# Windowed attention into a dropless MoE: one product a head for the values, and a different order of the copies and the routing around them

## The chip, the cores and the metric

One core of a Trainium2 chip runs the whole program. The metric is device time in microseconds of one execution; lower is better. Times come from separate runs, and one further execution was taken with the hardware profiler. Everything is float32.

## The reference, cut to what matters

```python
# attention: B, H, S, D = 4, 8, 768, 64; 8 memory keys a head; chunks of 32 queries
for c in range(S // 32):                 # each chunk sees its own 32 keys,
    l, r = max(0, 32*c - 16), min(S, 32*c + 32 + 8)   # 16 before, 8 behind
    k_full = concat(mem_k, k[:, :, l:r]); v_full = concat(mem_v, v[:, :, l:r])
    a = softmax(q_c @ k_full.T / sqrt(D))
    out[:, :, c] = a @ v_full
x = out.transpose(0, 2, 1, 3).reshape(B * S, H * D)    # 3072 tokens of 512
# mixture of experts: 8 experts, 512 -> 1024 -> 512
logits = x @ w_gate
e = argmax(logits); gate = softmax(logits)[e]
y[token] = gate * (relu(x[token] @ w1[e]) @ w2[e])
```

## The kernel before

**Stages.** Attention runs over 32 blocks `i` of 96 queries (8 blocks a batch entry). Behind it the last tokens are routed, while TensorE works on the first 256 tokens of expert 0 (`ph`, `py`), and then the eight experts follow, one after another, to the end. The change lies in the attention stage, in the first 140 us or so of the program.

**A block.** The 96 queries of a block see a window of 128 columns of `kT` (keys and the memory keys, which are copied in between). TensorE makes, in this order and written out by hand (`tc.manual_schedule`, one loop over `i` from line 1172):

1. `turn_q(i + 2)`: four transposes of q into a bank of PSUM (`tqk<-cst,qn`, line 544), then two copies by ScalarE into `qT` (line 661). Two blocks share one load of q: an even call turns the even heads of the pair of blocks, an odd call the odd heads. So what block `i` turns at an odd `i` is needed by the scores of block `i + 1`.
2. `scores(i)`: 16 products of 64 by 64 weights (`sc`, line 539), with keys on the partitions and queries along the row, then three exponentials by ScalarE, one for each chunk of 32 queries, into `ex` (line 713). `sc` has one buffer, so the next scores wait for these exponentials.
3. `values(i - 1, 0)` and `values(i - 1, 1)`: four heads each. The weights are the columns of `ex` (one per query), `v` with a column of ones is streamed (65 columns), and `o` gets the sums and the divisor. A head's 96 queries are taken as two products of 64 columns each (c = 0, 1), to partitions 0 to 63 and 64 to 127 of the bank. The second reaches 32 columns past the head, so `ex` is one tile with 32 zeroed columns at its end, in two fixed buffers, and the last 32 partitions of the bank aren't used. VectorE takes the reciprocal (line 730) and multiplies (line 732) into `xr`, the block's rows of x.
4. `turn_xb(i - 2)`: four transposes of x (`tx`) and a copy by ScalarE into a slice of a weight buffer (`w<-tx`, line 739), for the logits.
5. `turn_k(i + 4)`: four transposes of k (`tqk<-cst,kn`) and two copies by VectorE into `kT` (line 679; line 683 for the memory keys of a new batch entry).

Every four or five blocks (`GROUPS`) the logits of a finished group are made in the midst of the values (`o<-w,wg`), and its routing is put on a list `work` of small steps for VectorE (`top` to `where`), one product pair for TensorE (`rank`), the multiplication of x by the gate (GpSimd, line 843, for the first 22 blocks) and the scatters. `routing(n)` takes up to `n` VectorE steps from that list at its place in the block: 3 between the two halves of the values and 5 at the end of the block while i is below 24. A scatter (line 875, GpSimd, one per block of tokens) writes the rows of x to their experts' places in `x_dram`. Each is issued behind the TensorE instruction that stood last when it was written. `xr` has `NXR` = 12 buffers, and a block writes the one that the scatter of 12 blocks before has read.

**Queues.** SyncE issues all loads of q, k and v, in an order written out by hand three to six blocks ahead. Its waits are for buffers. A float32 product is two loads of weights and two matmuls in the trace; a transpose is one of each.

Of the kernel before, what the change touches and what calls it, by code (L numbers as in the profile page):

```python
# [10 lines left out]
F32 = mybir.dt.float32  # L11
# [8 lines left out]
B, H, S, D = 4, 8, 768, 64  # L20
NMEM = 8
CHUNK, LEFT, RIGHT = 32, 16, 8
QB = 96
NQB = S // QB
NB = B * NQB
# [43 lines left out]
PAIRS = QB  # L69
# [23 lines left out]
SIDE = max(t1 - t0 for t0, t1 in GROUPS)  # L93
EARLY = 22
BY_POOL = 22
NXR = 12


def can_be_plain(e):
# [433 lines left out]
def ordinary(ctx, tc, q, k, v, mem_k, mem_v, moe_w_gate, moe_w1, moe_w2, out, good):  # L533

    nc = tc.nc
    cur = {}

    def mm(*args, **more):
        i = nc.tensor.matmul(*args, **more)  # L539
        cur["pe"] = i.ins.name  # L540
        return i
# [18 lines left out]
    kpool = actx.enter_context(tc.tile_pool(name="kpool", bufs=1))  # L560
# [31 lines left out]

    qTs = [kpool.tile([128, H // 2, 2 * QB], F32, name=f"qT{i}") for i in range(NQ)]

    exs = [kpool.tile([128, H * QB + CHUNK], F32, name=f"ex{i}") for i in range(2)]
    for t in exs:
        nc.vector.memset(t[:, H * QB :], 0.0)
    vs = [kpool.tile([128, H, DV], F32, name=f"v{i}") for i in range(NV)]
    for t in vs:
        nc.gpsimd.memset(t[:, :, D], 1.0)  # L600
# [24 lines left out]
    sbs = [dict() for _ in range(NSB)]  # L625
# [21 lines left out]
    def turned_heads(t, n, x, bank=None):  # L647
        if bank is None:
            tt = ps_t.tile([128, H // 2, n], F32, tag="t", name="tqk")
        else:  # L650
            tt = bank[:, 0 : H // 2 * n].rearrange("p (a n) -> p a n", a=H // 2)
        for a in range(H // 2):
            turn(tt[:, a], t[0:n, 2 * a + x], ident[0:n, 0:n])
        return tt

    def turn_q(m, copy=nc.scalar.copy, bank=None):
        j, x = divmod(m, 2)
        tq = turned_heads(sbs[j]["qn"], PAIRS, x, bank)
        to = sbs[j]["qT"][D * x : D * x + D].rearrange("d a (p t) -> d a p t", t=2)
        for t in range(2):  # L660
            copy(to[:, :, :, t], tq[D * t : D * t + D])  # L661

    def turn_k(m, copy=nc.vector.tensor_copy, bank=None):
        j, x = divmod(m, 2)
        b, s = divmod(j, NSB // B)
        if s == 0 and x == 0:
            turned[b] = apool.tile([128, H // 2, KW], F32, name="kT")
        n = PAIRS + NMEM // 2 if s == 0 else PAIRS
        tk = turned_heads(sbs[j]["kn"], n, x, bank)
        half = turned[b][D * x : D * x + D]  # L670
        for t in range(2):
            of = tk[D * t : D * t + D]
            to = half[:, :, 2 * PER * s + t : 2 * PER * s + 2 * PER]
            to = bass.AP(
                tensor=to.tensor,
                offset=to.offset,
                ap=[list(to.ap[0]), [KW, H // 2], [PER, 2], [QB // 2 + NMEM, 2], [2, QB // 4]],
            )
            i = copy(to, of[:, :, 0:PAIRS].rearrange("d a (y z p) -> d a y z p", y=2, z=2))  # L679
            keyed.setdefault((b, s), []).append(i.ins.name)  # L680
            if s == 0:
                to = half.rearrange("d a (y c) -> d a y c", y=NQB)[:, :, :, QB // 2 : QB // 2 + NMEM]
                copy(
                    to.rearrange("d a y (p t) -> d a y p t", t=2)[:, :, :, :, t], bc(of[:, :, PAIRS:], 2, NQB)
                )

    def scores(i):
        s, (b, qb) = st[i], divmod(i, NQB)
        w0 = window(qb)
        sc = ps_s.tile([128, 2, 512], F32, tag="s", name="sc")  # L690
        for a in range(H // 2):
            for c in range(0, WIN, 64):
                for x in range(2):
                    rows = slice(D * x, D * x + D)
                    ins = mm(
                        sc[c : c + 64, x, QB * a : QB * a + QB],
                        lhsT=turned[b][rows, a, w0 + c : w0 + c + 64],
                        rhs=sbs[i // 2]["qT"][rows, a, QB * (i % 2) : QB * (i % 2) + QB],
                        start=True,
                        stop=True,  # L700
                    )
                    for z in range(NQB // 2):
                        if not w0 // (2 * PER) <= z <= (w0 + WIN - 1) // (2 * PER):
                            for j in keyed.get((b, z), []):
                                tc.declare_no_dep(ins.ins, j, reason="other keys")
        s["ex"] = exs[i % 2]
        ex = s["ex"][:, 0 : H * QB].rearrange("p (h t) -> p h t", h=H)
        x = 0 if qb == 0 else 2 if qb == NQB - 1 else 1
        sc4 = sc[:, :, 0 : 4 * QB].rearrange("p g (h t) -> p g h t", h=4)
        ex4 = ex.rearrange("p (h g) t -> p g h t", g=2)  # L710
        for g in range(3):
            sl = slice(CHUNK * g, CHUNK * g + CHUNK)
            nc.scalar.activation(  # L713
                ex4[:, :, :, sl], sc4[:, :, :, sl], AF.Exp, bias=mask[:, 3 * x + g : 3 * x + g + 1], scale=D**-0.5
            )

    def values(i, g, bank):
        s = st[i]
        if g == 0:
            s["x"] = xr[:, i % NXR, LB:DX]  # L720
        full = bank[:, 0 : 4 * (D + 1)].rearrange("p (h d) -> p h d", h=4)
        o = full[0:QB]
        for j in range(4):
            h = 4 * g + j
            for c in range(2):
                of = s["ex"][:, QB * h + 64 * c : QB * h + 64 * c + 64]
                mm(full[64 * c : 64 * c + 64, j], lhsT=of, rhs=s["v"][:, h, 0 : D + 1], start=True, stop=True)

        inv = inv_all[:, i, 4 * g : 4 * g + 4]
        nc.vector.reciprocal(inv, o[:, :, D])  # L730
        x = s["x"].rearrange("p (h d) -> p h d", h=H)
        nc.vector.tensor_tensor(x[:, 4 * g : 4 * g + 4], o[:, :, 0:D], bc(inv, 2, D), op=OP.mult)
# [170 lines left out]
    def routing(n, kinds="v"):  # L903
        while work and (n and work[0][0] in kinds or work[0][0] == "b"):
            kind, f = work.pop(0)
            f()
            n -= kind not in "sb"
# [6 lines left out]
    def scatter_some(n):  # L914
        while spread and n:
            spread.pop(0)()
            n -= 1

    def need(i, f, *lists):
        if 0 <= i < NB:  # L920
            f(i)
# [231 lines left out]
    with tc.manual_schedule():  # L1153
# [18 lines left out]
        for i in range(NB):  # L1172
            if i // 2 + 3 < NSB:
                (load_k, load_q)[i % 2](i // 2 + 3)
            need(i + 3, load_v)
            if i > 0:
                need(i + 2, turn_q)
            scores(i)
            if i == 0:
                need(i + 2, turn_q)  # L1180
            scatter_some(1)
            banks = [ps_o.tile([128, 512], F32, tag="o", name="o") for _ in range(2)]
            cur["bank"] = banks[0]
            if i <= 23:
                routing(1, "p")
            early_cnt = None
            if len(scatters) >= EARLY and "early" not in cur:
                cur["early"] = i
                early_cnt = early_counted(banks[0])
            if i >= 1:  # L1190
                values(i - 1, 0, banks[0])
            if early_cnt is not None:
                early_count(early_cnt)
            routing(5 if i > 23 else 3)
            done = [g for g in range(len(GROUPS)) if i - 3 == GROUPS[g][1] - 1]
            late = logits(done[0], banks[1]) if done else None
            if i >= 1:
                values(i - 1, 1, banks[1])
            need(i - 2, turn_xb)
            if late:  # L1200
                place_logits(*late)
            if i > 23:
                routing(1, "p")
            scatter_some(1)
            if i >= 24:
                routing(6)
            for m in {0: (), 1: (4, 5)}.get(i, (i + 4,)):
                need(m, turn_k)
            if i < 24:
                routing(5)  # L1210
            hold_back()
            for g in done:
                work.extend(routed(g))
            if i == 24:
                fetch_w(0, 4)
            if i >= 24:
                fetch_piece(1)
                fetch_piece(1)
            if i == 5:
                behind(  # L1220
                    nc.gpsimd.dma_start(
                        x_dram[0:TAIL].rearrange("(x p) c -> p x c", x=2), bc(zeros.bitcast(I32), 1, 2)
                    )
                )
                behind(nc.gpsimd.dma_start(x_dram[TAIL:NER], zeros[0 : NER - TAIL].bitcast(I32)))
            if i == 29:
                early_load()
                early_gather()
# [801 lines left out]
```

## Time and profile before

| | |
|---|---|
| timed runs | 470.24, 470.84, 476.84 us; median 470.84 |
| profiled execution | 474.63 us, of which the span is 472.5 |
| mean granted TensorE clock | 0.98 |
| TensorE busy | 439.4 us (93% of the span) |
| VectorE, ScalarE, GpSimd busy | 297.5, 195.3, 175.8 us |
| 60 to 120 us, per 20 us: TensorE | 17.66, 17.89, 19.05 us busy |
| the same: ScalarE | 13.30, 13.62, 14.23 us busy |
| the same: VectorE | 15.04, 15.15, 15.57 us busy |

A row of a profile that is in order of time has the start, the length, the engine, the line, the operation, out<-in, the shape (rows by columns of the weights, then partitions by streamed columns) and how many records were merged; in brackets stands an idle time of the engine before it and what ended it. PE is the matmul, PEld the load of weights that lies over it. "issue" is idle time in which the engine waited for nothing that the profile shows. The length of a matmul holds its way through the array, so the step between two rows is read from their starts.

### The profile page before, as it was taken

How to read it: one execution, taken by the hardware profiler on the slowest of the kernel's cores; microseconds unless marked ns; L12 is line 12 of the kernel's file. 1: busy time of each engine (PE TensorE's matmuls, PEld its weight loads, DVE VectorE, ACT ScalarE, POOL GpSimd, SP SyncE). 2: the span in 40 equal slices, each digit the busy share in tenths (PEclk: the TensorE clock that was granted, in tenths of full speed). 3: DMA queues.
4: the chain of work that ended last, by engine and by line, in shares of the span. 5: the costliest groups of instructions: out<-in, count | busy, mean ns of one | idle time of the engine just before them, and what ended most of it. 6: DMA issues, size and time to landing. Idle time of an engine off the chain costs nothing. (4 is left out here: it accounts for less than half of the span.)

```text
span 472.5 us, 11804 instructions
## 1 busy us (share of the span) xinstructions
PE 439.4 (93%) x4412; PEld 393.8 (83%) x4412; DVE 297.5 (63%) x572; ACT 195.3 (41%) x369; POOL 175.8 (37%) x211
## 2 busy tenths in 40 slices
PE   4799997999999899999999999999999999899992
PEld 4687786887778769999899999977888998879991
DVE  3476686787377586885476777765537977556410
ACT  3587675676532136421352254134213622135211
POOL 1010947877553206721414552232122333240124
PEclk9899999999799999999999999999999999999997
DMA  9999999999975686768895896594614979824002
GB/s 197 184 202 231 215 263 232 244 280 273 289 196 184 237 243 178 226 136 256 236 273 134 250 290 163 179 281 122 192 44 121 244 209 259 249 78 103 15 24 92
DMA packets 142239, 92.42 MB, mean 196 GB/s; under 512 B 79621, under 2 KB 125134, under 8 KB 142160
## 3 DMA queue, kind: packets, MB, share of 16 engines
q1 hardware_dynamic: 127504, 64.55, 57.5%
q10 hardware_dynamic: 7744, 13.24, 9.0%
q0 software_dynamic: 6912, 13.54, 8.2%
q8 instruction: 54, 0.88, 0.8%
q14 instruction: 25, 0.20, 0.2%
HBM read 65.68 MB, written 21.28 MB: 184 GB/s over the span
## 5 line engine op out<-in xcount | busy, mean ns | idle before, releaser
L1521 POOL DMA_INDIRECT out_dram<-y,lab x41 | 44.6, 1087 | 112.9 <-PE sum_q L539 43.6
L966 POOL DMA_INDIRECT lab<-x_dram,rows x42 | 52.0, 1239 | 65.0 <-PE sum_q L539 27.6
L539 PE MATMUL sum_p<-xsT,w 128*128 128x320 f32 (+8 forms) x256 | 53.7, 354 | 3.0 <-issue 1.9
L539 PEld LDWEIGHTS sum_p<-xsT,w 128*128 128x128 f32 x256 | 42.8, 190 | 9.8 <-issue 4.6
L539 PE MATMUL o<-v,ex 128*64 128x65 f32 x1024 | 43.7, 232 | 4.8 <-issue 4.8
L539 PEld LDWEIGHTS o<-v,ex 128*64 128x64 f32 x1024 | 36.4, 143 | 11.6 <-issue 8.5
L713 ACT ACTIVATE ex<-sc,cst 128x256 f32<-128x256 f32 x96 | 38.5, 471 | 12.9 <-PE sc L539 5.3
L1438 ACT COPY sum_r<-sum_p 128x640 f32<-128x640 f32 x36 | 24.4, 677 | 46.0 <-PE sum_p L539 40.1
L875 POOL DMA_INDIRECT x_dram<-xr,dest x32 | 29.9, 933 | 25.0 <-PE o L539 7.6
L539 PE MATMUL sum_q<-t,s 128*128 128x140 f32 (+5 forms) x192 | 36.7, 339 | 1.9 <-ACT sum_r L1438 1.9
L679 DVE COPY kT<-tqk 64x384 f32<-64x384 f32 x60 | 33.2, 554 | 7.9 <-PE tqk L544 6.7
L539 PE MATMUL sum_r<-t,w 128*128 128x140 f32 (+5 forms) x192 | 36.8, 339 | 0.0
L539 PE MATMUL sum_p<-t,s 128*128 128x140 f32 (+5 forms) x192 | 36.6, 339 | 0.0
L539 PEld LDWEIGHTS sum_q<-t,s 128*128 128x128 f32 x192 | 31.8, 193 | 5.5 <-issue 2.8
L539 PE MATMUL sum_p<-h,w 128*128 128x140 f32 (+5 forms) x192 | 35.6, 339 | 0.0
L730 DVE RECIPROCAL inv_all<-o 96x4 f32<-96x4 f32 x64 | 11.7, 183 | 37.4 <-PE o L539 27.6
L843 POOL TENSOR_SCALAR xr<-xr 96x512 f32<-96x512 f32 x22 | 34.1, 1557 | 0.2 <-DVE inv_all L730 0.2
L539 PEld LDWEIGHTS sum_p<-t,s 128*128 128x128 f32 x192 | 31.9, 193 | 2.2
L539 PEld LDWEIGHTS sum_p<-h,w 128*128 128x128 f32 x192 | 31.9, 195 | 2.2 <-issue 0.2
L539 PEld LDWEIGHTS sum_r<-t,w 128*128 128x128 f32 x192 | 31.8, 193 | 2.2
L661 ACT COPY qT<-tqk 64x384 f32<-64x384 f32 x60 | 30.4, 506 | 7.3 <-PE tqk L544 6.5
L1485 DVE STREAM_TRANSPOSE h<-yT 128x640 f32<-128x640 f32 x28 | 23.6, 841 | 14.7 <-DMA y<-h 14.2
(186 smaller groups left out, 800.7 us busy)
## 6 DMA issues: line engine op xcount, KB each, us to landing
w<-in_moe_w_dram SPq DMA_DIRECT2D x128, 128.0 KB
w<-in_moe_w_dram ACTq DMA_DIRECT2D x6, 2048.0 KB
xs<-x_dram SPq DMA_DIRECT2D x56, 160.0 KB
y<-h SPq DMA_DIRECT2D x112, 80.0 KB
kn<-in_k_dram SPq DMA_DIRECT2D x16, 384.0 KB
qn<-in_q_dram SPq DMA_DIRECT2D x16, 384.0 KB
x_dram<-zeros SPq DMA_DIRECT2D x8, 396.0 KB
v<-in_v_dram SPq DMA_DIRECT2D x24, 128.0 KB
```

The source lines that it names most:

```text
L539: i = nc.tensor.matmul(*args, **more)
L661: copy(to[:, :, :, t], tq[D * t : D * t + D])
L679: i = copy(to, of[:, :, 0:PAIRS].rearrange("d a (y z p) -> d a y z p", y=2, z=2))
L713: nc.scalar.activation(ex4[:, :, :, sl], sc4[:, :, :, sl], AF.Exp, bias=mask[:, 3 * x + g : 3 * x + g + 1], scale=D**-0.5)
L730: nc.vector.reciprocal(inv, o[:, :, D])
L843: return lambda: eng.tensor_scalar(x[:, LB:DX], x[:, LB:DX], x[:, 1:2], None, op0=OP.mult)
L875: i = nc.gpsimd.indirect_dma_start(out=x_dram, out_offset=bass.IndirectOffsetOnAxis(ap=dest[:, t : t + 1], axis=0), in_=xr[:, t % NXR].bit ...
L966: return nc.gpsimd.indirect_dma_start(out=to.bitcast(I32), out_offset=None, in_=x_dram.rearrange("r (k c) -> (r k) c", c=LB), in_offset=ba ...
L1438: op("ACT", one_op(lambda: nc.scalar.copy(to, of)), reads, writes)
L1485: op("DVE", one_op(lambda: nc.vector.transpose(to, of)), [("y", m, y)], [("yr", m, y), "y00"], upto=upto)
L1521: return nc.gpsimd.indirect_dma_start(out=out, out_offset=bass.IndirectOffsetOnAxis(ap=which.bitcast(I32), axis=0), in_=y, in_offset=None, ...
```

## The change

- In `values`, a head's 96 queries are one product with 96 columns of weights instead of two with 64. `ex` becomes an ordinary tile of a pool with two buffers, without the zeroed end.
- `turn_q` is split. The transposes stay where they were, before the scores; the two copies (`keep_q`) are written behind the block's exponentials.
- In `turn_k`, of an odd call from the seventh on, the second of the two key copies goes to ScalarE.
- `routing` takes 2 and 3 steps a block instead of 3 and 5 while i is below 24.
- `xr` has 14 buffers.

```diff
-NXR = 12
+NXR = 14
...
-    exs = [kpool.tile([128, H * QB + CHUNK], F32, name=f"ex{i}") for i in range(2)]
-    for t in exs:
-        nc.vector.memset(t[:, H * QB :], 0.0)
...
     def turn_q(m, copy=nc.scalar.copy, bank=None):
+        keep_q(m, turned_heads(sbs[m // 2]["qn"], PAIRS, m % 2, bank), copy)
+
+    def keep_q(m, tq, copy=nc.scalar.copy):
         j, x = divmod(m, 2)
-        tq = turned_heads(sbs[j]["qn"], PAIRS, x, bank)
...
-            i = copy(to, of[:, :, 0:PAIRS].rearrange("d a (y z p) -> d a y z p", y=2, z=2))
+            eng = nc.scalar.copy if t and m % 2 and m > 5 else copy
+            i = eng(to, of[:, :, 0:PAIRS].rearrange("d a (y z p) -> d a y z p", y=2, z=2))
...
-        s["ex"] = exs[i % 2]
-        ex = s["ex"][:, 0 : H * QB].rearrange("p (h t) -> p h t", h=H)
+        ex = s["ex"] = apool.tile([128, H, QB], F32, name="ex")
...
-        full = bank[:, 0 : 4 * (D + 1)].rearrange("p (h d) -> p h d", h=4)
-        o = full[0:QB]
+        o = bank[0:QB, 0 : 4 * (D + 1)].rearrange("p (h d) -> p h d", h=4)
         for j in range(4):
             h = 4 * g + j
-            for c in range(2):
-                of = s["ex"][:, QB * h + 64 * c : QB * h + 64 * c + 64]
-                mm(full[64 * c : 64 * c + 64, j], lhsT=of, rhs=s["v"][:, h, 0 : D + 1], start=True, stop=True)
+            mm(o[:, j], lhsT=s["ex"][:, h], rhs=s["v"][:, h, 0 : D + 1], start=True, stop=True)
...
-            if i > 0:
-                need(i + 2, turn_q)
+            tq = None
+            if 0 < i < NB - 2:
+                tq = turned_heads(sbs[(i + 2) // 2]["qn"], PAIRS, i % 2)
             scores(i)
             if i == 0:
                 need(i + 2, turn_q)
+            if tq is not None:
+                keep_q(i + 2, tq)
...
-            routing(5 if i > 23 else 3)
+            routing(5 if i > 23 else 2)
...
             if i < 24:
-                routing(5)
+                routing(3)
```

On TensorE, from the end of block 7 on, there stands before:

```order
L544 MATMUL tx<-cst,xr 128x96 x4
L544 MATMUL tqk<-cst,kn 128x96 x4
L544 MATMUL tqk<-cst,qn 128x96 x4
L539 MATMUL sc<-qT_102,kT 64x96 x16
L539 MATMUL o<-v_109,ex_105 64x65 x16
L544 MATMUL tx<-cst,xr 128x96 x4
L544 MATMUL tqk<-cst,kn 128x96 x4
L544 MATMUL tqk<-cst,qn 128x96 x4
```

and with the change:

```order
L544 MATMUL tx<-cst,xr 128x96 x4
L544 MATMUL tqk<-cst,kn 128x96 x4
L544 MATMUL tqk<-cst,qn 128x96 x4
L539 MATMUL sc<-qT_102,kT 64x96 x16
L539 MATMUL o<-v_105,ex 96x65 x8
L544 MATMUL tx<-cst,xr 128x96 x4
L544 MATMUL tqk<-cst,kn 128x96 x4
L544 MATMUL tqk<-cst,qn 128x96 x4
```

(64x65 and 96x65 are partitions by columns of the result.) The order of TensorE's steps is the same, the products for logits and ranks included; 16 products of a block's values have become 8.

On ScalarE, blocks 9 to 11, before (`ex` the exponentials, `qT` the copies of q, `w<-tx` the copy of x):

```order
L739 COPY w_131<-tx 128x4x96
L661 COPY qT_103<-tqk 64x384 x2
L713 ACTIVATE ex_105<-sc,cst 128x2x4x32 x3
L739 COPY w_131<-tx 128x4x96
L661 COPY qT_102<-tqk 64x384 x2
L713 ACTIVATE ex_104<-sc,cst 128x2x4x32 x3
L739 COPY w_131<-tx 128x4x96
L661 COPY qT_102<-tqk 64x384 x2
L713 ACTIVATE ex_105<-sc,cst 128x2x4x32 x3
```

and with the change:

```order
L712 ACTIVATE ex<-sc,cst 128x2x4x32 x3
L660 COPY qT_103<-tqk 64x384 x2
L735 COPY w_127<-tx 128x4x96
L679 COPY kT<-tqk 64x4x2x2x24
L712 ACTIVATE ex<-sc,cst 128x2x4x32 x3
L660 COPY qT_102<-tqk 64x384 x2
L735 COPY w_127<-tx 128x4x96
L712 ACTIVATE ex<-sc,cst 128x2x4x32 x3
L660 COPY qT_102<-tqk 64x384 x2
```

In each block the copies of q have moved from in front of the exponentials to behind them, and every second block has a key copy behind the copy of x.

## The prediction

> **What bounds the kernel now.** I read the page first (engine shares), then the attention stage alone, because every edit lies in it: the waits in its window, one undisturbed block of it in order of time, and one disturbed block.
>
> ```profile
> span 472.5 us, 11804 instructions
> PE 439.4 (93%) x4412; PEld 393.8 (83%) x4412; DVE 297.5 (63%) x572; ACT 195.3 (41%) x369; POOL 175.8 (37%) x211
> ```
>
> PE is the bound of the whole. In time order, one block of attention (block 14, from its scores `sc` to the next block's):
>
> ```profile
> 63.75 0.89 PE L539 MATMUL sc<-qT,kT 64*64 64x96 f32 x32
> 64.57 1.15 PE L539 MATMUL o<-v,ex 128*64 128x65 f32 x32
> 65.66 0.55 PE L544 MATMUL tx<-cst,xr 96*128 96x96 f32 x4
> 66.04 0.49 PE L544 MATMUL tqk<-cst,kn 96*128 96x96 f32 x4
> 66.37 0.49 PE L544 MATMUL tqk<-cst,qn 96*128 96x96 f32 x4
> 66.80 0.31 PE L539 MATMUL sc<-qT,kT 64*64 64x96 f32 x4
> ```
>
> First column start, second length. No row has an idle bracket: PE runs 0.82 us of scores, 1.09 of values (`o`), 0.38, 0.33 and 0.43 of transposes, 3.05 us a block, and waits for nobody. So here a longer or shorter PE row moves the block by as much. ScalarE in the same block:
>
> ```profile
> 64.20 1.02 ACT L661 COPY qT<-tqk 64x384 f32<-64x384 f32 x2
> 65.25 1.20 ACT L713 ACTIVATE ex<-sc,cst 128x256 f32<-128x256 f32 x3
> 66.33 0.49 ACT L739 COPY w<-tx 128x384 f32<-128x384 f32 x1
> ```
>
> It has 2.71 us of work in 3.05. The waits of the stage, by the window 10 to 145:
>
> ```profile
> PEld o L539 <- issue: 11.6, 28, 1.6
> PEld tqk L544 <- issue: 4.1, 6, 2.4
> PE tqk L544 <- DMA qn<-in_q_dram: 2.2, 1, 2.2
> PEld tx L544 <- issue: 1.6, 3, 0.7
> PE sc L539 <- ACT ex L713: 0.3, 1, 0.3
> ```
>
> Columns: total us, times, longest. TensorE hardly waits for ScalarE (0.3) and for VectorE not at all; what it loses is "issue", time in which no semaphore holds it. Of 4.1 + 1.6 + 11.6, the one of 2.4 is the load of q shown below it, and the seven logits steps have a regular idle of about 0.25 each (1.7). About **13 us of stalls** are left. What they look like, in block 17:
>
> ```profile
> 75.83 0.49 PE L544 MATMUL tqk<-cst,qn 96*128 96x96 f32 x4
> 75.87 0.99 POOL L875 DMA_INDIRECT x_dram<-xr,dest  x1 [0.17 <-POOL xr L843]
> 76.26 0.89 PE L539 MATMUL sc<-qT,kT 64*64 64x96 f32 x32
> 77.08 0.45 PE L539 MATMUL o<-v,ex 128*64 128x65 f32 x7
> 77.16 0.92 POOL L875 DMA_INDIRECT x_dram<-xr,dest  x1 [0.30 <-issue]
> 77.87 0.38 PE L539 MATMUL o<-v,ex 128*64 128x65 f32 x5 [0.35 <-issue]
> 77.89 0.22 PEld L539 LDWEIGHTS o<-v,ex 128*64 128x64 f32 x4 [0.50 <-issue]
> 78.64 0.82 PE L539 MATMUL o<-v,ex 128*64 128x65 f32 x20 [0.39 <-issue]
> 79.39 0.30 PE L544 MATMUL tx<-cst,xr 96*128 96x96 f32 x1
> ```
>
> In the middle of a group, where nothing is waited for, TensorE gets some 8 instructions (4 loads, 4 products) in 0.76 us and then runs on; `o` takes 2.31 us (77.08 to 79.39) for 1.09. It looks like a shortage of instructions. The stall begins just behind a scatter of GpSimd (77.16) that meets the densest stretch of code; the scatter at 75.87, among transposes, cost nothing.
>
> **The change, part by part.** *Values, one product a head.* Each head had two products with 64 columns of weights, side by side; it gets one with 96 columns. Each product is two records of load and two of matmul, so a block's 32 + 32 records become 16 + 16. The trace shows both widths in one place, at full clock: the small late logits load 96 columns and stream only 8.
>
> ```profile
> 139.92 0.82 PE L539 MATMUL o<-wg,w 128*96 128x8 f32 x8
> 140.66 0.69 PE L539 MATMUL o<-v,ex 128*64 128x65 f32 x16
> 141.28 0.48 PE L539 MATMUL ph<-x0T,w 128*128 128x256 f32 x1
> 139.89 0.76 PEld L539 LDWEIGHTS o<-wg,w 128*96 128x96 f32 x8
> 140.66 0.55 PEld L539 LDWEIGHTS o<-v,ex 128*64 128x64 f32 x16
> L539 PEld LDWEIGHTS o<-wg,w x24: 159/165/165, 139.9 to 148.5; 128*96 128x96 f32 x24
> L539 PEld LDWEIGHTS o<-v,ex x992: 132/138/232, 20.0 to 141.1; 128*64 128x64 f32 x199
> ```
>
> Eight loads of 96 columns fill 0.76 us with the last one's 0.165 in it: a step of (0.76 - 0.165)/7 = **0.085 us**. Sixteen of 64 step (0.55 - 0.138)/15 = 0.0275, so a pair takes 0.055. A group of four heads, entry and exit included, took 0.62 (140.66 to 141.28) with 16 narrow records; eight wide ones took 0.74 (139.92 to 140.66), of which 0.74 - 7 x 0.085 = 0.145 is the way in and out. Sixteen wide records in a row are then 15 x 0.085 + 0.145 = 1.42 us against 1.09: **+0.33 a block**. What has no row is a 96-column load with 65 columns streamed. Its bounds: nothing (the wide step equals the pair's) and 2 x 0.74 - 1.09 = +0.39; I take +0.33, by the nearest row. There are 32 blocks of values; the first lies under the load of q that PE waits 2.2 us for, so 31 x 0.33 = **+10.2 us** (0 to +12.5).
>
> A rule of the skill bears on this price. The Trainium skill, "TensorE: Matmul & The Clock Gate", section "LDWEIGHTS (loading the stationary operand)", has a load last its columns over 1.2 in ns, whatever the rows. By it 96 columns cost an estimated 80 ns against 53 for 64 that run side by side, which speaks against the change, and the sum by it (27 ns a step, 15 steps, 31 blocks) would be 1.4 us below mine; the row above agrees to 5 ns.
>
> *Fewer instructions against the stalls.* The scores ask for 64 instructions in 0.82 us and the values for 64 in 1.09, 59 per us; after the change the values ask for 32 in 1.42, 23 per us. Transposes ask for 8 in 0.33, 24 per us, and it was among transposes that the scatter cost nothing. Values should become as patient as these; the scores stay dense. A block's instructions fall from 152 (64, 64, and 24 for transposes) to 120. Bounds: 0 (a stall is a fixed outage) and -13 (all go). A scatter that falls before or into the scores still finds the queue drained there, so I take seven tenths, **-9.2 us**.
>
> *The clock.* A slow stretch follows the stalls of 122 to 125:
>
> ```profile
> 116.70:125.20 8.50, 7.39 (x171) 5.95 (x170) 4.04 (x11) 4.92 (x11) 6.95 (x6) 1.00 1.02 277
> 125.20:132.00 6.80, 6.79 (x105) 5.89 (x105) 3.44 (x18) 3.27 (x8) 1.87 (x6) 0.50 0.62 205
> 125.87 1.56 PE L539 MATMUL sc<-qT,kT 64*64 64x96 f32 x32
> 127.87 2.00 PE L539 MATMUL o<-v,ex 128*64 128x65 f32 x32
> 129.80 0.90 PE L544 MATMUL tx<-cst,xr 96*128 96x96 f32 x4
> 130.63 1.54 PE L539 MATMUL sc<-qT,kT 64*64 64x96 f32 x32
> ```
>
> In the first two rows the column behind the five engines is the granted clock: 0.50 for 6.8 us, after a stretch in which PE idled 1.1 us. Against the lengths in the undisturbed block the two scores cost 0.67 and 0.65 more, the values 0.85, the transposes 0.35: 2.5 us. If the stalls ahead of it shrink, it need not come. I take two thirds, **-1.7** (0 to -2.5; a new drop elsewhere would cost as much).
>
> *q's copies behind the exponentials; a key copy in four by ScalarE.* Now the exponentials wait for the copies (64.20 to 65.22) though the scores ended at 64.64. Swapped, they can run from about 64.74 to 65.94, and the copies to 66.96. In every odd block those copies are the half of q that the next block's scores need; TensorE, with 1.42 for the values, gets there at 66.80 + 0.33 = 67.13. They stay covered, by 0.17 us; if that cover goes, the next scores wait, some 0.1 us in 15 blocks, 1.5 in all. Queued behind them are `w` (0.49) and, in odd blocks, the key copy (about 0.5); the next exponentials need ScalarE at 67.13 + 0.98 = 68.11, and it is done at about 67.9. I take 0 (0 to +1.5).
>
> *Routing over more blocks, 14 buffers.* VectorE's small steps move back by up to a block, but TensorE's rank products and GpSimd's scatters stay in the same blocks. PE waits for neither engine in the list above, so 0; the early part of the first expert, which follows without a gap, starts as much earlier or later as attention ends.
>
> **Sum**: +10.2 - 9.2 - 1.7 + 0 = -0.7 us. The profiled execution took 474.63 us (472.5 of span, 2.1 around it), so it would take 473.9. It is 3.8 above the median of the three timed runs, 470.84; the difference put on the median gives 470.1, and I say **470**. (The timed runs may hold fewer of the stalls than the profiled one, and so have less to win; that lies inside the range.) Two per cent of 470.84 is 9.4 us, about what a measurement of this kernel can tell from no change.
>
> **The rivals.** *S, slower: the stalls don't care for density.* If each is a fixed outage behind a scatter, the rarer instructions wait just as long, the slow clock comes too, and the wide loads are paid in full: +10.2, so 481.0. For it: stalls also stand in front of transposes (the 4.1 and 1.6 above). Against it: the free scatter at 75.87. It decides as soon as less than a tenth of the 13 us goes. The Trainium skill, "Runtime: NRT & Kernel Launch", section "Instruction fetch mechanics", says that code streams in by blocks and that crossing one is mostly hidden; by that rule thinner code buys nothing, which is this rival's result. The gaps inside a group speak against it.
>
> *F, faster: the wide load is cheaper than the row.* Transposes load 128 columns quicker:
>
> ```profile
> 65.96 0.39 PEld L544 LDWEIGHTS tqk<-cst,kn 96*128 96x128 f32 x4
> ```
>
> (0.39 - 0.14)/3 = 0.083 us a load of 128 columns, so 96 of that kind would step at 0.062, and a block's values would take 15 x 0.062 + 0.145 = 1.08, no more than now. Then -9.2 - 1.7 leaves 459.9. Against it: the 0.085 is measured on a plain product of the same 96 columns, and a transpose is one record where a product is two.
>
> *N: the change doesn't thin anything that matters*, because TensorE turns out to wait for something else in each block (ScalarE's chain of 0.98 + 1.20 + 1.02 at odd blocks). That is S's price with 1.5 more, 482.5, and I count it with S.
>
> **How the numbers follow.** Forecast 0.72, S with N 0.16, F 0.09, anything else 0.03. The forecast's own range: four tenths to all of the stalls (-5.3 to -13), clock 0 to -2.5, values +9.3 to +12.1, so 464 to 478. To leave out no more than 2 in 10 it must reach S at 481; F is left out. Range 464 to 481. Faster by over 2% is F and the low end of the forecast, 0.11; slower by over 2% is the part of S and N above 480.3, 0.14; the rest, 0.75, lies within.
>
> **What would show it.** Values of 1.4 us in an undisturbed block, 0.085 a step, and a block of 3.4 us: the first term. "issue" in front of `o` down from 11.6 us to about 4: the second. No stretch at 0.50 between 100 and 140: the third. Exponentials beginning 0.1 us behind the scores, and PE still not waiting for `qT`: the fourth. I am wrong if the wide step is far from 0.085, if the stalls keep their total, or if `sc` begins to wait for ScalarE.

## The result, and the profile after

Over 20 executions of each, the kernel before took 474.73 us (median) and the changed one 480.23: a ratio of 1.0135, 95% interval 1.0104 to 1.0167. It is **slower by 6.4 us**. The forecast, next to no change (-0.7 us, 470), had the wrong sign; that 480.23 lies within its range (464 to 481) is no merit of the forecast, because the upper end was set for the rival S. Executions that are much longer than the others of their kernel are left out of the ratios, and the profiles of the values alone, the old routing, 14 buffers with a pad and 12 buffers fell in such executions, so sums of waits from those four are less sure.

The page and the waits in 10 to 145 us, of the changed kernel:

```profile
span 477.9 us, 10765 instructions
PE 444.5 (93%) x3900; PEld 403.2 (84%) x3900; DVE 289.2 (61%) x556; ACT 200.8 (42%) x382; POOL 175.5 (37%) x210
PEld tqk L544 <- issue: 4.5, 4, 1.9
PE tqk L544 <- DMA qn<-in_q_dram: 3.4, 2, 1.7
PEld o L539 <- issue: 2.4, 9, 0.5
PE tqk L544 <- DMA kn<-in_k_dram: 1.1, 2, 0.7
PE o L539 <- DVE xr L839: 1.0, 1, 1.0
PE tqk L544 <- DMA kn<-in_mem_k_dram: 0.6, 1, 0.6
PE o L539 <- DMA v<-in_v_dram: 0.5, 1, 0.5
```

(One line per waiter and releaser: us in all, times, longest; these are the lines that the text uses.) The "issue" in front of the values fell from 11.6 us to 2.4, further than forecast. New are waits for loads (3.4 + 1.1 + 0.6 + 0.5 = 5.6 us, where before only q's 2.2 and k's 0.3 stood) and for VectorE. From block 10, in order of time:

```profile
51.61 1.55 PE L539 MATMUL o<-v,ex 128*96 128x65 f32 x16
53.00 0.50 PE L544 MATMUL tx<-cst,xr 96*128 96x96 f32 x4
53.34 0.49 PE L544 MATMUL tqk<-cst,kn 96*128 96x96 f32 x4
53.67 0.49 PE L544 MATMUL tqk<-cst,qn 96*128 96x96 f32 x4
```

The values take 1.39 us to the next step (1.09 before), the four transposes behind them 0.34 (0.38 before). The clock of the changed kernel behind block 27:

```profile
121.40:124.80 3.40, 3.40 (x35) 2.77 (x34) 0.60 (x2) 1.60 (x4) 1.41 (x2) 0.50 0.92 278
124.80:135.00 10.20, 8.83 (x160) 7.79 (x159) 6.81 (x30) 6.27 (x15) 3.53 (x10) 1.00 0.99 288
135.00:138.40 3.40, 3.40 (x38) 3.05 (x37) 0.88 (x4) 0.00 (x0) 1.31 (x2) 0.50 1.15 201
138.40:141.80 3.40, 2.76 (x30) 2.42 (x28) 1.37 (x3) 0.96 (x2) 0.13 (x1) 0.99 0.90 253
141.80:145.20 3.40, 2.96 (x7) 2.42 (x8) 3.04 (x18) 0.22 (x1) 2.68 (x3) 0.51 0.91 285
```

The 0.50 (the column behind the five engines) did not go; behind block 27 it stands in three pieces of 3.4 us, where one of 6.8 stood before. And in the stage that I had not looked at as one, from the last scores to the first product of the experts, by windows (start and end, length, busy time of PE, PEld, DVE, ACT and POOL, clock, share of the transfers, GB/s), before:

```profile
134.00:174.40 40.40, 38.15 (x301) 30.47 (x300) 27.66 (x108) 8.72 (x23) 13.91 (x22) 1.00 0.71 222
```

and changed:

```profile
132.40:176.70 44.30, 40.73 (x268) 33.09 (x267) 27.00 (x106) 8.57 (x22) 14.49 (x23) 0.92 0.78 236
```

Block 31 began 1.6 us earlier than before, and the experts' products 2.3 later. The other 3.1 us of the 5.4 by which the two spans differ lie behind that, in the experts, where nothing was changed: from their first product to the end all the profiles below have between 298 and 302 us. One pair of profiles can't say which edit cost what; the runs do.

### The profile page after: what moved, and what is told of

Its sections match the earlier page's. It is cut to its first block, busy times and chain, and to the rows that moved or that the text cites. A ratio compares the mean times of both kernels' runs of the same rounds, so it can differ in the third digit from the quotient of the medians.

```text
span 477.9 us, 10765 instructions
## 1 busy us (share of the span) xinstructions
PE 444.5 (93%) x3900; PEld 403.2 (84%) x3900; DVE 289.2 (61%) x556; ACT 200.8 (42%) x382; POOL 175.5 (37%) x210
## 5 line engine op out<-in xcount | busy, mean ns | idle before, releaser
L539 PE MATMUL o<-v,ex 128*96 128x65 f32 x512 | 53.2, 255 | 1.2 <-DVE xr L839 1.0
L539 PEld LDWEIGHTS o<-v,ex 128*96 128x96 f32 x512 | 47.8, 168 | 6.4 <-issue 2.4
L726 DVE RECIPROCAL inv_all<-o 96x4 f32<-96x4 f32 x64 | 11.2, 176 | 41.1 <-PE o L539 40.6
L679 DVE COPY kT<-tqk 64x384 f32<-64x384 f32 x47 | 25.9, 550 | 9.3 <-PE tqk L544 8.6
```

Source lines behind the costliest of these rows:

```text
L679: i = eng(to, of[:, :, 0:PAIRS].rearrange("d a (y z p) -> d a y z p", y=2, z=2))
```

## The experiments

My theory after the traces (A): the values' edit pays for itself, and the other edits lose the time, behind block 27. Its rival (B): the wide loads cost more than the stalls give back. Ratios are to runs of the kernel before on the same chip.

**Halves.** The values alone:

```diff
-            for c in range(2):
-                of = s["ex"][:, QB * h + 64 * c : QB * h + 64 * c + 64]
-                mm(full[64 * c : 64 * c + 64, j], lhsT=of, ...)
+            mm(o[:, j], lhsT=s["ex"][:, QB * h : QB * h + QB], rhs=s["v"][:, h, 0 : D + 1], start=True, stop=True)
```

> The kernel before with one 96-column product a head as its only edit. Theory A (the wide load was sized well and the thinner code does lose the stalls; what the changed kernel lost, it lost behind block 27, by the other edits: work of VectorE and loads that come later): values 1.42 us a block, in-group idle before the values falls from 11.6 to under 3 us, time 472 to 476 against 474.7, ratio 0.995 to 1.003. Theory B (the wide load costs more than the stalls give back, whatever the rest does): 479 to 482, ratio 1.01 to 1.016, with the same stretch from block 31 to the end of the span as the changed kernel.

Measured 476.59, ratio 1.0007 (0.996 to 1.0054); "issue" before the values 4.4 us. All other edits (the same diff, turned back in the changed kernel):

> The changed kernel with two 64-column products a head as before (and the two fixed buffers for ex): all other edits alone. Theory A: stalls as before (11 to 13 us inside groups), values 1.09 us a block, and the loss behind block 27 is here as in the changed kernel: 477 to 481, ratio 1.005 to 1.013. Theory B: the other edits are free or gain a little: 470 to 475, ratio 0.99 to 1.001.

Measured 481.96, ratio 1.0146 (1.0101 to 1.0191), with most of the stalls still there (7.8 us of "issue" before the values, 3.7 before the scores). **A holds, B falls**: the values' edit, on which most of my working went, costs nothing that can be measured, and the edits that I had costed at 0 cost 6.9 us. A's place for the loss does not hold: block 31 begins at 139.6 us in this profile, 5.6 later than before, and the stretch from there to the experts is as long as before (40.4 us), so this version loses its time in attention.

**The other edits one by one**, each in the kernel before. q's copies behind the exponentials:

> The kernel before with q's copies issued behind the exponentials as its only edit. All edits but the values cost 6.9 us together, the routing none of it by itself. If q's order makes it (the half of q for the next block is ready later, so TensorE stands in front of the scores in odd blocks, 0.2 to 0.4 us in 15 blocks): 478 to 482 against 475, ratio 1.007 to 1.015, and waits of the scores for qT of 2 us or more. My prediction, which costed it at 0 to +1.5: 475 to 476.5, ratio 1.000 to 1.003.

Measured 474.32, 0.9972 (0.9937 to 1.0007): free. The key copies:

> The kernel before with one key copy in four by ScalarE as its only edit. If this makes the 6.9 us (each copy puts 0.5 us into ScalarE's chain ahead of the next exponentials): 478 to 482, ratio 1.007 to 1.015, TensorE waiting for ex or kT. By the prediction, nothing: 474 to 476, ratio 0.998 to 1.003.

Measured 475.78, 1.0004 (0.9968 to 1.0041): free. It is a warning too: its profile has 3.7 us of scores waiting for the exponentials (`sc` for `ex`, before 0.3), and the time didn't move, so a wait of some us in one profile is no loss yet. The buffers:

```diff
-NXR = 12
+NXR = 14
```

> The kernel before with 14 buffers for x instead of 12 as its only edit. If this makes the 6.9 us (nothing in the attention waits for these buffers before the change, so only by memory laid out otherwise or by scatters that run further behind): 478 to 482, ratio 1.007 to 1.015. By the prediction, nothing: 474 to 476, ratio 0.998 to 1.003.

Measured 479.32, 1.0087 (1.005 to 1.0125): **4.1 us** from a number that no wait in the profile spoke of. And the routing:

```diff
-            routing(5 if i > 23 else 3)
+            routing(5 if i > 23 else 2)
...
-                routing(5)
+                routing(3)
```

> The kernel before with the routing spread as in the change (2 and 3 steps a block up to block 23 instead of 3 and 5) as its only edit. The other edits together cost 5.7 us even with kn and qn on multiples of 512, though q's order, the key copy and 14 buffers cost nothing each. If the routing makes it (its scatters come in unbroken runs of four or five later in the block, and all engines stall there): 479 to 483, ratio 1.007 to 1.015, with a stop of some 5 us in one block between 17 and 20. If it is free, as predicted: 474 to 477, ratio 0.997 to 1.004.

Measured 480.98, 1.0089 (1.0056 to 1.0121): **4.2 us**. Its complement, all edits but the values and the routing (the buffers with a pad, explained below):

> All edits but the values and the routing (q's copies behind the exponentials, the key copy in four by ScalarE, 14 buffers with kn and qn on multiples of 512). If q's order and the key copy cost only together (both lengthen ScalarE's chain in odd blocks, 3.2 us in a block of 3.05): 479 to 483, ratio 1.007 to 1.015, TensorE waiting 2 us or more for ex and qT. If the routing makes the loss: 473 to 476, ratio 0.994 to 1.001.

Measured 478.24, 1.0019 (0.9984 to 1.0055): q's order and the key copy cost nothing together either. Added up, the five edits alone make +0.3 - 1.3 + 0.2 + 4.1 + 4.2 = +7.5 us, against 6.4 measured for all; the four without the values make 7.2, against 6.9. Each of these five figures is uncertain by some 2 us.

**Where the routing's cost may show.** One of the routing's steps does not run on VectorE alone: behind its subtraction (`lg`, L804) comes an exponential on ScalarE (L805), in ScalarE's queue ahead of the block's exponentials. Its rows in the kernel before:

```profile
43.78 0.24 ACT L805 ACTIVATE lg<-lg 96x40 f32<-96x40 f32 x1 [0.42 <-DVE lg L804]
63.70 0.24 ACT L805 ACTIVATE lg<-lg 96x40 f32<-96x40 f32 x1 [0.18 <-DVE lg L804]
80.29 0.23 ACT L805 ACTIVATE lg<-lg 96x32 f32<-96x32 f32 x1 [0.20 <-DVE lg L804]
96.44 0.23 ACT L805 ACTIVATE lg<-lg 96x32 f32<-96x32 f32 x1 [0.19 <-DVE lg L804]
```

and with the routing's edit alone:

```profile
44.54 0.24 ACT L805 ACTIVATE lg<-lg 96x40 f32<-96x40 f32 x1 [1.27 <-DVE lg L804]
66.25 0.24 ACT L805 ACTIVATE lg<-lg 96x40 f32<-96x40 f32 x1 [1.38 <-DVE lg L804]
83.91 0.23 ACT L805 ACTIVATE lg<-lg 96x32 f32<-96x32 f32 x1 [1.51 <-issue]
98.95 0.23 ACT L805 ACTIVATE lg<-lg 96x32 f32<-96x32 f32 x1 [1.95 <-issue]
```

The bracket is ScalarE's idle time in front of it: 0.2 us became 1.3 to 2.0. The third of them in order of time:

```profile
82.53 1.13 DVE L679 COPY kT<-tqk 64x384 f32<-64x384 f32 x2
83.69 0.19 DVE L804 TENSOR_TENSOR lg<-lg,ltop 96x32 f32<-96x32 f32 x1
83.91 0.23 ACT L805 ACTIVATE lg<-lg 96x32 f32<-96x32 f32 x1 [1.51 <-issue]
84.04 0.99 ACT L661 COPY qT<-tqk 64x384 f32<-64x384 f32 x2
85.06 1.20 ACT L713 ACTIVATE ex<-sc,cst 128x256 f32<-128x256 f32 x3
86.32 0.40 PE L539 MATMUL sc<-qT,kT 64*64 64x96 f32 x8 [1.59 <-ACT ex L713]
```

With portions of 3 the subtraction was the third step of the first portion and stood ahead of the two key copies; with portions of 2 it comes behind them (1.13 us). ScalarE waits for it, with q's copies and the exponentials queued behind, and TensorE waits 1.59 us for the scores' bank. In this profile that makes 4.4 us in 5 places:

```profile
PE sc L539 <- ACT ex L713: 4.4, 5, 1.6
```

That it equals the 4.2 us is no proof: the key copies' run had 3.7 for nothing, the complement, which costs nothing, has an idle time of 2.76 us in front of this exponential, and the "issue" moved too (11.6 to 4.9 us before the values, 0.7 to 7.3 before the scores). In the changed kernel the first two of these wait 1.15 and 0.59 us, with the exponentials behind it and q's copies behind those.

The cause that the expectation named is there as well. The moved routing bunches the scatters: block 18 has three of them where it had two, and lasts 6.9 us where it lasted 4.1 (though blocks 16 to 18 together last 14.1 against 14.4). Of the eight profiles with the new routing seven have 6.9 to 8.9 us in block 18 (the changed kernel itself 3.3), the twelve others 3.0 to 5.4. Which of the two makes the 4.2 us, the runs do not separate.

**The buffers: by work or by address.** Nothing in the kernel waits for these buffers; but two more of them move all that lies behind them in the core's memory. `kn` and `qn`, where k and q land in pieces of 512 bytes, begin on a multiple of 512 before, 128 past one with 14 buffers, and 384 past one in the changed kernel. The address alone:

```diff
     xr = kpool.tile([QB, NXR, DX], F32, name="xr")
+    kpool.tile([QB, 32], F32, name="pad")
```

> The kernel before with 128 bytes a partition left unused behind xr as its only edit, so that the landing buffers of k and q (kn, qn) and all behind them begin 128 bytes past a multiple of 512, as they do with 14 buffers for x. Layout theory (the 512-byte pieces of k and q land slower at such addresses, and the loads, whose queue is busy through all of attention, hold TensorE up): median of a 512-byte piece 41 to 47 ns in 14 to 44 us against 36, 478 to 481, ratio 1.006 to 1.012. Rival (it is the 14 buffers themselves, by later scatters or another order of the steps): 474 to 477, ratio 0.997 to 1.003, pieces at 36 ns.

Measured 481.95, 1.0118 (1.0072 to 1.0165): **5.6 us for 128 bytes that nobody uses**. The median piece of 512 bytes took 42 ns in 14 to 44 us, 36 before. And 14 buffers with a pad of 96 values instead, so that the address is a multiple of 512 again:

> The kernel before with 14 buffers for x and 384 unused bytes behind them, so that kn and qn begin on multiples of 512 again. Layout theory: 473 to 477, ratio 0.995 to 1.003, 512-byte pieces at 36 ns. Rival (the 14 buffers themselves): 478 to 481, ratio 1.006 to 1.012, as without the unused bytes.

Measured 475.54, 0.9983 (0.9951 to 1.0015). So it is the layout and not the buffers. The length of a piece goes with the address in all of these nineteen profiles: its median in 14 to 44 us is 27 to 40 ns in the thirteen with `kn` and `qn` on a multiple of 512, 41 to 44 in the six where they lie 128 or 384 bytes past one. How that becomes time is less clear. The queue of the loads in 14 to 44 us (packets, MB, share of 16 engines), before:

```profile
q1 hardware_dynamic: 15613, 5.56, 104.4%
```

with the 128 bytes:

```profile
q1 hardware_dynamic: 14912, 5.29, 106.6%
```

and with 14 buffers:

```profile
q1 hardware_dynamic: 14327, 5.08, 108.7%
```

Fewer bytes in more engine time: the loads move 5 to 9% less. But with 14 buffers and the pad it is 5.18 MB and 40 ns a piece, so the times show that the address matters and the traces don't settle how the loss is made.

**The changed kernel with each of its costs taken out.** The routing in the old portions:

> The changed kernel with the routing taken in the old portions (3 and 5 steps a block up to block 23 instead of 2 and 3), all else as changed. If the later routing makes the loss behind block 27 (VectorE still busy with it, labels and loads late): TensorE's waits for VectorE from block 28 to the first expert go, time 476 to 478 against the changed kernel's 480. If the routing is free, as predicted: 480 to 481, ratio to before as the changed kernel's, 1.012 to 1.015.

Measured 484.31, 1.0142 (1.0089 to 1.0194): nothing regained. The address:

> The changed kernel with 128 unused bytes behind xr, so that kn and qn, which it has 384 bytes past a multiple of 512, begin on one. Layout theory: the whole loss is this, so 473 to 476 against 475 before, ratio 0.993 to 1.002, 512-byte pieces at 36 ns instead of 44. Rival (the loss is made by the edits' new order of work, late in attention): 478 to 481, ratio 1.008 to 1.014.

Measured 486.57, 1.0197 (1.0151 to 1.0242): worse, though the pieces took 36 ns. With 12 buffers:

> The changed kernel with 12 buffers for x; kn and qn then begin 256 bytes past a multiple of 512. Layout theory: half the distance is still off, 477 to 481, ratio 1.004 to 1.012 (or, if only odd multiples of 128 are slow, 473 to 476). Rival (the 14 buffers themselves): 474 to 477 whatever the address.

Measured 483.7, 1.0094 (1.0053 to 1.0135), with pieces of 35 ns, as on a multiple of 512: by this one profile, 256 bytes off does not slow them, and 128 or 384 does. And the edits without the values, with the address restored:

> All edits but the values (two narrow products a head as before, 14 buffers), with 384 unused bytes that put kn and qn on multiples of 512. Layout theory: the 6.9 us that these edits cost go, 472 to 476, ratio 0.992 to 1.001. Rival (the order of the edits costs something of its own): 478 to 482, as without the unused bytes.

Measured 481.24, 1.012 (1.0073 to 1.0167), with pieces of 29 ns. The single runs add up to +2.3 us for it, and 5.7 were measured. Without the pad it was 1.0146, so here the address gives back no more than the intervals allow. The routing does: this version and the complement above (1.0019, 0.9984 to 1.0055) differ in the routing's portions alone, and the intervals do not meet, so **the routing's cost shows a second time, some 4.8 us, among the other edits.** (In that pair block 18 goes from 5.3 to 8.5 us, and the scores' waits for the exponentials from none to 1.5.) With wide products neither cost can be taken out one at a time. There the clock may stand in the way. The window rows of the changed kernel with the address restored:

```profile
17.10:20.50 3.40, 1.90 (x43) 1.70 (x44) 1.85 (x4) 0.43 (x2) 0.00 (x0) 1.00 1.17 181
20.50:37.60 17.10, 17.10 (x176) 15.98 (x174) 6.78 (x19) 7.85 (x19) 0.00 (x0) 0.50 1.11 196
37.60:92.20 54.60, 51.21 (x885) 46.12 (x880) 32.13 (x113) 39.12 (x91) 27.79 (x34) 1.00 0.96 221
```

against the kernel before:

```profile
16.00:19.40 3.40, 1.17 (x29) 0.90 (x31) 2.32 (x5) 0.96 (x3) 0.00 (x0) 1.00 1.15 192
19.40:22.80 3.40, 3.40 (x58) 3.06 (x50) 1.20 (x4) 1.84 (x5) 0.00 (x0) 0.50 1.14 182
22.80:26.20 3.40, 3.40 (x83) 3.10 (x82) 2.20 (x6) 2.92 (x7) 0.00 (x0) 1.00 1.14 195
```

Both wait some 2 us for q at 17 us and fall to 0.50 behind it. With narrow products the clock is back after one stretch of 3.4 us; with wide ones after five. So it is in every profile that has a fall there, 19 to 22 us into the program: 3.4 us in all eight with narrow products; 23.9 with the values alone and 23.9 with the old routing, 17.1 here, 13.7 with 12 buffers. The profile of the changed kernel itself has no fall there, but its 20 executions have a mean granted clock of 0.975, its variants with wide products 0.978 to 0.981, the versions of the other edits with narrow ones 0.984 to 0.987, the values alone 0.986, the kernel before 0.979 to 0.990 in its five sets. To test it, the wait was filled, with seven products that nobody reads:

```diff
+            if i == 2:
+                fill = ps_t.tile([128, 128], F32, tag="t", name="fill")
+                for _ in range(7):
+                    mm(fill, lhsT=ones, rhs=ones, start=True, stop=True)
```

> The changed kernel with kn and qn on multiples of 512 bytes, and seven products of 128 by 128 ones (their result is read by nobody) where TensorE waits for the load of q ahead of block 2. Clock theory: the granted clock falls to 0.50 after a stretch of 3.4 us in which the array has too little work (columns streamed times the share of rows and columns used, under some 1400), and with one wide product a head attention at 0.50 has some 1200 to 1420 in such a stretch, so it stays there for 14 to 24 us; two narrow products have more and come back after 3.4. With the wait filled: no 0.50 between 17 and 40 us, 475 to 480 where the same kernel without the products had 486.6. Rival (the 486.6 comes from the address or the order of the edits, the clock being a symptom): 484 to 488, unchanged.

> The kernel before with the same seven products in the wait ahead of block 2. Clock theory: it has 0.50 for one stretch of 3.4 us there and loses under 2 us by it, so 473 to 476, ratio 0.994 to 1.001. Rival (filling the wait helps any version, by 6 us or more): 467 to 470, ratio 0.982 to 0.989.

> The same with the seven products in the wait ahead of block 2: the version that should be the fastest if both theories hold. 470 to 475, ratio 0.988 to 0.998; if one of them fails, 476 to 481.

Measured 484.24, 1.0139 (1.0067 to 1.0211), for the changed kernel with the address restored; 475.7, 0.9994 (0.9956 to 1.0033), for the kernel before; 480.38, 1.0126 (1.0087 to 1.0165), for the edits without the values. The 0.50 at 20 us was gone in all three. The kernel before did as the clock theory has it; the other two came out where their second ranges are, those for a theory that fails. The wide version came down from 1.0197 to 1.0139, which is within the intervals; its profile then has 13.7 us at 0.50 from 83.5 us on, behind a stop in block 18. So filling this one wait gains nothing that can be measured, and what share of the wide version's loss the clock makes is not shown.

**Scatters and stalls.** To see whether a scatter stalls TensorE only where it meets dense code, the scatters up to block 24 were released behind the second half of the values, one a block, and none behind the scores:

> The kernel before, with up to block 24 one scatter a block, released behind the second half of the values (so that it falls among the transposes), and none behind the scores; from block 25 on as before. Density theory (a scatter that falls into scores or values starves TensorE, one among transposes does not): in-group idle before values and scores in blocks 11 to 24 falls from some 7 us to under 2, time 467 to 470, ratio 0.985 to 0.992. Rival (a stall comes with each scatter, or with the code's position, wherever the scatter falls): idle and time unchanged, ratio 0.997 to 1.003.

Measured 491.54, 1.0294 (1.0242 to 1.0347). VectorE waited 15.4 us for `x_dram`: the scatters now lag behind the 12 buffers that they empty. With 14:

> The kernel with scatters only among transposes up to block 24, now with 14 buffers for x, because with 12 VectorE waited 15.4 us for scatters that came late. Density theory: in-group stalls in blocks 11 to 24 gone, nobody waiting for the scatters, 467 to 471, ratio 0.985 to 0.993. If the scatters' lateness still costs (VectorE waiting for x_dram): over 480. Rival (stalls go with each scatter or with the code's position): stalls unchanged, 473 to 477, ratio 0.997 to 1.003.

Measured 480.7, 1.0087 (1.0045 to 1.0128), the same as 14 buffers without the move; both carry the shifted address. The "issue" before the values is 11.5 us, but 5.1 of it is one wait for a load of v at 136 us. In 45 to 110 us it is 3.4 us, against 7.1 in the kernel before and 3.0 with 14 buffers alone: fewer stalls, and not by the move. This part of my theory is not confirmed. What a stall is, a run of rows shows better, from the edits without the values with the address restored:

```profile
78.90 0.92 POOL L879 DMA_INDIRECT x_dram<-xr,dest  x1 [0.30 <-issue]
80.12 0.92 POOL L879 DMA_INDIRECT x_dram<-xr,dest  x1 [0.31 <-issue]
80.62 0.38 PE L539 MATMUL sc<-qT,kT 64*64 64x96 f32 x3 [0.93 <-issue]
80.67 0.55 DVE L683 COPY kT<-tqk 64x384 f32<-64x384 f32 x1 [1.88 <-remote]
81.25 0.49 ACT L683 COPY kT<-tqk 64x384 f32<-64x384 f32 x1 [1.82 <-issue]
81.35 0.92 POOL L879 DMA_INDIRECT x_dram<-xr,dest  x1 [0.30 <-issue]
83.48 0.32 PE L539 MATMUL sc<-qT,kT 64*64 64x96 f32 x2 [1.12 <-issue]
```

In a run of scatters not only TensorE stops: VectorE and ScalarE stand idle for 1.9 and 1.8 us. The signals in the trace say what they wait for. VectorE's copy waits for TensorE's signal of the key transposes; these ended at 78.46, the signal was set at 80.64, and the copy begins at 80.67. ScalarE's copy waits for VectorE's and begins at 81.25, behind its end at 81.22. So the engines stand because TensorE's signal comes 2.2 us late; what holds it up is not shown.

## Why the prediction was wrong, point by point

- **"PE is the bound ... and waits for nobody."** True of a block, not of the stage. I read the shares of the engines and not the row of the page below them:

```profile
DMA  9999999999975686768895896594614979824002
```

The transfers are busy in nine tenths or more through the first 130 us. Where TensorE loses little by stalls, it meets them, as in the run with q's order alone:

```profile
PEld o L539 <- issue: 5.7, 9, 2.5
PE o L539 <- DMA v<-in_v_dram: 5.0, 3, 2.3
PE tqk L544 <- DMA qn<-in_q_dram: 4.1, 2, 2.4
PE tqk L544 <- DMA kn<-in_k_dram: 0.8, 1, 0.8
```

It waited 9.9 us for loads, against 2.5 before. (4.1 of the 5.7 us are the same waits for v, seen by the load of weights; 1.6 us are left, in seven short pieces.) This fits two bounds close together, so that a stall removed is partly a wait for a load gained, and what slows the loads (128 bytes) costs at once.

- **Values, +10.2.** Mechanism and step were right (1.39 us against the 1.42 worked out); the four transposes behind them gave back 0.04 us, so a block went from 3.05 to 3.32, and the term was 31 x 0.27 = 8.4.
- **Stalls, -9.2.** In front of the values as forecast (11.6 to 4.4 with the edit alone, "about 4"), but in front of the scores they rose from 0.7 to 2.6: -5.3 in sum. I had said that the scores stay dense, and yet took seven tenths of the whole. Among the other edits, wide against narrow products gave 2.6 against 11.5 (the changed kernel), 9.1 against 12.5 (address restored) and 8.4 against 10.9 (wait filled). So the sum was lower each time, by 2.5 to 8.9. That thinner code is the reason is not shown: with q's order alone, and values as dense as before, the stalls before the values are all but gone too (the 1.6 us above), and the key copies' run has 3.6. Of 8.4 - 5.3 = +3.1 the run shows +0.3 (-1.9 to +2.6); the small rest is open.
- **Clock, -1.7.** Not gained: in attention both profiles have 10.2 us at 0.50, and the mean clock of the changed kernel's executions is 0.975, the lowest of these versions but for the one with late scatters (0.965). The wide products make it harder to leave 0.50.
- **q's copies and key copies, 0.** Right, alone (0.9972, 1.0004) and together (1.0019).
- **"Routing over more blocks, 14 buffers ... PE waits for neither engine in the list above, so 0."** This is the step that failed: 4.2 and 4.1 us, each as the only edit. I read that nobody waits for VectorE in the kernel before and took it as cover for any delay. But the routing's subtraction brings an instruction on ScalarE, in front of the exponentials, and I followed only VectorE and GpSimd; and the scatters did not stay in their blocks (block 18 has three instead of two). Which of these makes the 4.2 us stays open. The buffers I judged by who waits for them and not by what they move in memory.
- **"... starts as much earlier or later as attention ends."** In the profiled pair it did not: 1.6 us earlier, then 2.3 later, with two of the three stretches at 0.50 in between. The other profiles bear this out. Where block 31 begins at 134.0 us or later, the experts follow it by 38.8 to 40.6 us (16 profiles); where it begins earlier, by 44.3 to 48.1 (the changed kernel, q's order alone, and 14 buffers with and without the moved scatters). With q's order alone block 31 came 7.0 us earlier than before and the experts 1.7. In three of these four TensorE waits 4.2 to 6.1 us for loads of v there, so time that attention gains is mostly not passed on.
- **Rivals.** The time landed beside S (481.0) by luck. S stood on 470.84, the median of three runs, where 20 give 474.73; as a difference it meant +10.2, and 6.4 were measured, for another reason: the stalls did shrink. N's place, ScalarE's chain, was near the routing's cost, but at the logits' exponential and not at q's copies.

What stays open: why the changed kernel regains nothing when the routing or the address is taken back, and how much of that is the clock; by what the address slows the loads; whether the routing costs by the exponential or by the bunched scatters; what makes TensorE's signals late.

## What to carry to other kernels

Follow every instruction that a moved step issues onto every queue, and ask what stands behind it there: a small exponential that waits for a delayed VectorE step holds up the large ones behind it. Read the row of the transfers before calling an engine the bound, since where both are close, removed stalls can come back as waits for loads, and see whether the next stage can start any earlier. And when a buffer count changes, look where the tiles behind it begin; a pad of a few bytes is a one-line test of that, and each edit of a bundle wants its own run.

## What the runs showed of the hardware

- **The granted clock follows the work in the array more closely than its busy time.** Count in each stretch of 3.41 us the columns streamed, each weighted with the used share of the 128 x 128 array, over the attention of 20 profiles. Of 82 stretches at 0.50, all 38 with more than 1,467 were followed by full clock, none of the 12 with less than 1,204; no stretch at full clock with more than 1,422 was followed by 0.50. (Here a product is spread over its length; counted whole at its start, the marks are 1,517, 1,158 and 1,508.) By the profile, in which the ends of products are modelled, PE was busy all of the time in slow ones (17.10 of 17.10 us above). A block has 768 for scores and 864 for transposes, and 1,040 for narrow values but 780 for wide ones, since 96 columns are loaded once where 128 were used. At 0.50 a wide block lasts 6.19 us (30.68 to 36.87 with the values alone) and so has 1,330 a stretch, between those marks; that fits its staying there for several stretches. The Trainium skill, "TensorE: Matmul & The Clock Gate", section "Part 1: The HAM clock gate (the "warmup" mystery)", has a free-running window of 3413 ns after which a busy array gets its full clock: the lengths agree (3.4, 6.8, 10.2, 13.7, 17.1, 23.9 us), but five such windows of a TensorE that is wholly busy by the profile, at half clock, show that this is not enough.
- **128 unused bytes a partition in front of the landing buffers cost 1.2%** (1.0072 to 1.0165) in the kernel before, and pieces of 512 bytes take 41 to 44 ns instead of 27 to 40; 384 bytes past a multiple of 512 did the same, 256 (35 ns) did not. Among the other edits the time did not come back with the address.
- **In a stall TensorE's signals come late.** In an undisturbed block of the kernel before, each is set 0.02 to 0.05 us behind the end of its product (64.64 and 64.69, 65.26 and 65.28). In block 18 of the run with the routing alone, amid a run of scatters, five steps ended at 77.89, 78.36, 78.84, 79.17 and 79.50, and the five signals were set at 79.54, 81.84, 81.90, 81.96 and 82.02; VectorE and ScalarE begin right behind them (79.56, 81.86, 81.92). That the scatters make them late is not shown.
